# A retention layer and a bilinear feed-forward on one core: seven products for the first tile's last outputs, and an order changed around it

## The chip, the cores and the metric

The kernel runs on one core of a Trainium2 chip. A time is the device time of one execution in microseconds (us); the median of three executions is given. Beside it stands one execution that the hardware profiler recorded, with the start and length of every instruction. Engines are named as the profile names them: PE is TensorE's matmul, PEld its weight load, DVE is VectorE, ACT is ScalarE, POOL is GpSimd, and SP issues the DMAs. All times in the text are counted from the first instruction of the profiled execution, its span.

## The reference

For each of 4 x 8 heads a state of 64 x 64 decays by the head's factor gamma and takes in the outer product of k and v, and q reads it. The result, 3072 tokens of 512 features, goes through two weights whose outputs are multiplied, and through a third weight.

```
state = gamma * state + outer(k[t], v[t]);  y[t] = (q[t] @ state) / 8
x = y as [3072, 512]
out = ((x @ w_a) * (x @ w_b)) @ w_out        # 512 -> 1536 -> 512, float32 in and out
```

## The kernel before

The 768 steps of a sequence are cut into 6 chunks of 128, so there are 24 slots of 128 tokens. The recurrence becomes matmuls: q and k are scaled by a table of powers of gamma, `scores` makes their products within a chunk, a mask cuts them, `intra` applies them to v, `update` adds a chunk to the state, `inter` lets q read it. The first six slots go as three pairs (`casts2`, `flip2`, `scores2`, `update2`, `intra2`, `inter2`, `leave2`): their q and k are transposed on TensorE. From slot 6 on, `casts(t)` scales k and q on GpSimd (`scaled`, L239), casts v (L206), issues a transposing DMA on SP's queue (L254) and then the loads of slot t + 2 (L94, L99). `turn(new, old)` puts scores and state of the slots new, new + 1 and the reads of old, old + 1 on TensorE.

The outputs of the slots are the input of the feed-forward, in tiles of 4, 2, 2, 2, 2, 4 and 8 slots (J = 0 to 6). A tile's 12 blocks of 128 hidden features are each an `a` (L462, w_a, evicted to bf16 by ScalarE, L465) and a `g` (L472, w_b), four matmuls each; VectorE multiplies the two into `ht` (L474). PSUM has three banks under the name `ff` for them. The weights come in six slices that GpSimd casts to bf16 (`cast_w`).

The outputs of a tile come in one of two ways. `ffn_out` (L493) makes one row block of 128 tokens by 12 matmuls of 512 columns. `Group` and `single` make two row blocks together by 7 products of half blocks in place of 8, each of six matmuls of 256 columns (L561), and need sums and differences of the hidden features (`hsum`: `hs` 1 to 4, L503) and of the third weight (`weight_sums`: T1 to T4, L503). TensorE's snapshots of partial sums go out by ScalarE (L568), and VectorE adds them. Before, tile 0 uses the plain way for its four blocks, the later tiles the other. The last tile uses the same seven products for its first two weights too (`Unit`, L698), from sums of the weights that GpSimd makes piece by piece (`weight_pieces`).

Every instruction is chained to the one before on its engine by `seq`, so that the order of the text is the order of each engine's and each DMA queue's work; what is written for different engines runs beside each other, held by semaphores alone. Buffers come from pools with a fixed count (three raw buffers each for k, q and v, three for `kqT`, six `w`), and a load into one waits until its last reader is done. `warm` (L448) multiplies zeros, with no reader, to fill time early on.

Around the change the text before reads (L828 to L836, and L889 to L905):

```
    cast_w(0); W2 = 2 * P
    warm(psff, "ff", 256)
    intra2(1, 0, True); inter2(1)
    ffn_a(0, 0, 0, W2)
    intra2(1, 1, False); leave2(1, (A_, D_))
    ffn_a(0, 1, 0, W2)
    ...
    casts(6); blocks(1, 0, 3); casts(7); blocks(1, 3, NFT)
    outs(0, 0); weight_sums(0, 3); weight_sums(3, 6); outs(0, 1)
    casts(8); outs(0, 2); turn(6, None, V_)
    hsum(1, 3, 0, 6); hsums(1, 0, 6, V_)
    outs(0, 3); casts(9); turn(None, 6); single(1, AT0, AT1, FF)
```

Of the kernel before, what the change touches and what calls it, by code (L numbers as in the profile page):

```python
# [16 lines left out]
PAIRS = 3  # L17


LOADS = "p0 p1 w0 w1 w2 w3 w4 k2 q2 a5 v2 b5 o0 o1 o2 o3 o4 o5 s6 s7".split()  # L20


@with_exitstack
def kernel(
# [10 lines left out]
    nc = tc.nc  # L35
# [44 lines left out]

    raws, wst, whole = {}, {}, {}

    def load_slot(t):
        b, ci = divmod(t, NCH)
        for nm, src in (("k", k), ("q", q), ("v", v)):
# [38 lines left out]
    def issue_loads(n):  # L124
        for _ in range(min(n, len(pending))):
            what = pending.pop(0)
            n = int(what[1:])
            if what[0] in "ab":
                load_w(n, what[0])
            elif what[0] in "kqv":  # L130
                load_two(what[0], {"k": k, "q": q, "v": v}[what[0]], 0, n, 2 * n)
            else:
                {"p": load_pair, "s": load_slot, "w": load_w, "o": load_o}[what[0]](n)


    kqb = {}
# [65 lines left out]
    def cast(engine, dst, src):  # L202
        if engine is nc.scalar:
            seq(nc.scalar.copy(dst, src))
        else:
            seq(engine.tensor_copy(dst, src))  # L206
# [238 lines left out]
    def warm(pool, tag, *cols):  # L445
        idle = pool.tile([P, HP * P], F32, tag=tag, name="idle")
        for n in cols:
            seq(nc.tensor.matmul(idle[:, :n], zero[:, :P], zero[:, :n], start=True, stop=True,  # L448
                                 skip_group_check=True))
# [17 lines left out]
    def ffn_g(J, ft, c0=0, c1=None):  # L467
        c1 = TILES[J] * P if c1 is None else c1
        fs = slice(ft * P, (ft + 1) * P)
        g = psff.tile([P, 4 * P], F32, tag="ff", name="g")[:, : c1 - c0]  # L470
        for kt in range(KT):
            seq(nc.tensor.matmul(g, wb_bf[:, kt, fs], xcols(J, kt, c0, c1),  # L472
                                 start=(kt == 0), stop=(kt == KT - 1)))
        seq(nc.vector.tensor_tensor(ht[J][:, ft, c0:c1], g, asbs.pop((J, ft, c0)), op=ALU.mult))  # L474
# [13 lines left out]
    def ffn_out(J, i):  # L488
        store()
        osb = osbp.tile([P, DM], F32, tag="osb", name="osb")  # L490
        o = psff.tile([P, DM], F32, tag="ff", name="o")
        for ft in range(NFT):
            seq(nc.tensor.matmul(o, ht[J][:, ft, i * P : (i + 1) * P], wo_bf[:, ft],  # L493
                                 start=(ft == 0), stop=(ft == NFT - 1)))
        cast(nc.scalar, osb, o)
        held.append((rows(J, i // 2, i % 2), osb))

    def rows(J, u, r):
        n0 = (sum(TILES[:J]) + 2 * u) * P
        return out[n0 : n0 + 2 * P, :].rearrange("(n r) d -> r n d", r=2)[r]  # L500

    def tt(dst, x, y, op, eng=nc.vector):
        seq(eng.tensor_tensor(dst, x, y, op=op))  # L503

    T1 = []

    def weight_sums(a, b):
        if not T1:
            T1.append(wstage.tile([P, NP, DH], BF16, tag="w", name="wsum1"))
        j = slice(a, b)  # L510
        tt(T3[:, j], B22[:, j], B12[:, j], ALU.subtract)
        tt(T2[:, j], T3[:, j], B11[:, j], ALU.add)
        tt(T4[:, j], B21[:, j], T2[:, j], ALU.subtract)
        tt(T1[0][:, j], B12[:, j], B11[:, j], ALU.subtract)

    hs = {}

    def hsum(J, s, a, b, eng=nc.vector):
        U = 2 if isinstance(J, tuple) else TILES[J] // 2
        if (J, s) not in hs:  # L520
            pool, tag = (raw, ("kf", "qf", "vf", "kf")[s - 1]) if J == (BIG, 1) else (wstage, "w")
            hs[J, s] = pool.tile([P, NP, 2, P], BF16, tag=tag, name=f"hs{s}")
        v = ht[J].rearrange("p (k j) (u r n) -> p r k j u n", k=2, r=2, n=P)
        A11, A12, A21, A22 = (v[:, r, k2, a:b, :U] for r in range(2) for k2 in range(2))
        S = {x: hs[J, x][:, a:b, :U] for x in (1, 2, 3, 4) if (J, x) in hs}
# [335 lines left out]
    scores2(2, 0, "y")  # L861
    scores2(2, 1)
    ffn_a(0, 10)
    update2(2, 0)
    ffn_a(0, 11)
    intra2(2, 0, True)
    inter2(2)
    intra2(2, 1, False)
    leave2(2, (A_, D_))
    ffn_g(0, 10)  # L870
    ffn_g(0, 11)
    for j in range(NO):
        cast_o(j)
# [65 lines left out]
    v_cast(14)  # L939
# [67 lines left out]
```

## Time and profile before

| what | us |
|---|---|
| median of 3 executions (222.5 to 222.67) | 222.5 |
| the profiled execution | 222.53 |
| its span, first to last instruction | 220.8 |
| PE busy in it | 214.2 |
| POOL busy | 140.6 |
| DVE busy | 135.8 |
| ACT busy | 99.2 |

A row of the order of time gives the start in us, the length in us, the engine, the line, the operation, what it writes and reads, the shapes, how many instructions were merged (x4), and in brackets how long the engine stood idle before and what it waited for. Matmuls are pipelined: a row's length holds the drain of its last matmul, and the next row starts before it ends, so the price of a piece is the distance of two starts, or its length in the chain of waits, where overlaps are cut off. A row of the waits gives who waited for what: us in total, how often, the longest. A row of DMA issues gives how many, the KB of each and the median us from issue to landing.

### The profile page before, as it was taken

How to read it: one execution, taken by the hardware profiler on the slowest of the kernel's cores; microseconds unless marked ns; L12 is line 12 of the kernel's file. 1: busy time of each engine (PE TensorE's matmuls, PEld its weight loads, DVE VectorE, ACT ScalarE, POOL GpSimd, SP SyncE). 2: the span in 40 equal slices, each digit the busy share in tenths (PEclk: the TensorE clock that was granted, in tenths of full speed). 3: DMA queues.
4: the chain of work that ended last, by engine and by line, in shares of the span. 5: the costliest groups of instructions: out<-in, count | busy, mean ns of one | idle time of the engine just before them, and what ended most of it. 6: DMA issues, size and time to landing. Idle time of an engine off the chain costs nothing.

```text
span 220.8 us, 5622 instructions
## 1 busy us (share of the span) xinstructions
PE 214.2 (97%) x2233; PEld 144.6 (66%) x2244; DVE 135.8 (61%) x254; ACT 99.2 (45%) x217; POOL 140.6 (64%) x155
## 2 busy tenths in 40 slices
PE   7999999999999999999999999999999999999994
PEld 3567445587458878878888665456865444448883
DVE  3785347745774473566476345776465777789642
ACT  3364333443224444354576344555536656542331
POOL 5364666777554469659846944599999999820000
PEclk9999999999999999999999999999999999999999
DMA  6999999997999999999998599990022000000055
GB/s 170 290 324 348 350 309 342 385 262 164 217 186 286 214 239 240 237 180 274 188 224 219 118 245 194 225 174 3 3 85 105 0 1 3 0 1 4 24 190 166
DMA packets 87194, 39.68 MB, mean 180 GB/s; under 512 B 57472, under 2 KB 82944, under 8 KB 87168
## 3 DMA queue, kind: packets, MB, share of 16 engines
q1 hardware_dynamic: 87024, 39.26, 76.9%
q8 instruction: 17, 0.28, 0.5%
q14 instruction: 9, 0.07, 0.1%
q10 hardware_dynamic: 144, 0.07, 0.1%
HBM read 28.31 MB, written 6.29 MB: 157 GB/s over the span
## 4 chain that ended last, share of the span: by engine, by line
PE 93%; DMA 2%; DVE 2%; issue 1%; ACT 0%; SPq 0%; DVEq 0%; ACTq 0%
PE a L462 19%; PE g L472 19%; PE mA L561 12%; PE uA L698 8%; PE mB L561 6%; PE o L493 5%; PE uB L698 4%; PE mC L561 3%; DMA qf<-in_q_dram 2%; PE at L273 2%; PE y L320 2%; PE uC L698 2%; PE st L290 2%; PE kb L756 2%; PE ka L756 2%; PE y L427 1%
## 5 line engine op out<-in xcount | busy, mean ns | idle before, releaser
L474 DVE TENSOR_TENSOR ht<-g,asb 128x256 bf16<-128x256 f32 (+1 forms) x74 | 37.1, 503 | 40.4 <-PE g L472 34.0
L472 PE MATMUL g<-xt,wb_bf 128*128 128x256 bf16 (+1 forms) x296 | 53.2, 304 | 0.4 <-DVE ht L474 0.4
L462 PE MATMUL a<-xt,wa_bf 128*128 128x256 bf16 (+1 forms) x292 | 53.4, 304 | 0.2
L465 ACT CAST asb<-a 128x256 bf16<-128x256 f32 (+1 forms) x74 | 32.2, 437 | 44.6 <-PE a L462 42.0
L472 PEld LDWEIGHTS <-wb_bf 128*128 128x128 bf16 x296 | 28.8, 98 | 13.4 <-issue 0.7
L239 POOL TENSOR_TENSOR kqb<-kf,ktab 128x512 bf16<-128x512 f32 x22 | 23.2, 1057 | 20.4 <-DMA kf<-in_k_dram 17.3
L462 PEld LDWEIGHTS <-wa_bf 128*128 128x128 bf16 x296 | 27.9, 98 | 12.2 <-issue 0.8
L561 PEld LDWEIGHTS <-hs 128*128 128x128 bf16 x240 | 23.4, 98 | 3.9
L279 DVE TENSOR_TENSOR aT<-at,mask 128x512 bf16<-128x512 f32 x36 | 22.3, 683 | 0.3
L704 ACT COPY snap<-uA 128x512 f32<-128x512 f32 x30 | 16.7, 588 | 12.6 <-PE uA L698 12.0
L239 POOL TENSOR_TENSOR kqb<-qf,qtab 128x512 bf16<-128x512 f32 x18 | 19.2, 1066 | 4.7 <-DMA qf<-in_q_dram 4.7
L503 POOL TENSOR_TENSOR hs<-ht,hs 128x384 bf16<-128x384 bf16 (+1 forms) x17 | 16.6, 982 | 5.8 <-DVE ht L474 5.8
L568 ACT COPY snaps<-mA 128x256 f32<-128x256 f32 x30 | 11.2, 373 | 19.8 <-PE mA L561 19.7
L561 PEld LDWEIGHTS <-ht 128*128 128x128 bf16 x180 | 17.5, 98 | 2.8
L503 POOL TENSOR_TENSOR hs<-ht 128x384 bf16<-128x384 bf16 (+2 forms) x12 | 13.8, 1152 | 3.7 <-DVE ht L474 3.7
L561 PE MATMUL mA<-wsum,hs 128*128 128x256 bf16 x120 | 15.7, 273 | 0.0
L206 POOL CAST vb<-vf 128x512 bf16<-128x512 f32 x16 | 10.1, 643 | 7.3 <-DMA vf<-in_v_dram 7.1
L503 POOL TENSOR_TENSOR ht<-gsb,asb 128x512 bf16<-128x512 bf16 x12 | 13.9, 1169 | 1.3 <-DVE gsb L503 1.3
L503 DVE TENSOR_TENSOR osb<-mB,snaps 128x256 f32<-128x256 f32 x20 | 8.4, 422 | 9.4 <-PE mB L561 5.1
L493 PE MATMUL o<-wo_bf,ht 128*128 128x512 bf16 x46 | 10.6, 380 | 0.1
L331 ACT CAST xt<-y 128x512 bf16<-128x512 f32 x18 | 9.7, 588 | 1.5 <-PE y L320 1.4
L448 PE MATMUL idle<-zero 128*128 128x256 f32 (+2 forms) x16 | 8.2, 632 | 1.6 <-DVE zero L140 1.5
(104 smaller groups left out, 323.0 us busy)
## 6 DMA issues: line engine op xcount, KB each, us to landing
qf<-in_q_dram SPq DMA_DIRECT2D x12, 512.0 KB, 5.7
out_dram<-osb SPq DMA_DIRECT2D x21, 256.0 KB, 3.9
kf<-in_k_dram SPq DMA_DIRECT2D x18, 256.0 KB, 4.6
vf<-in_v_dram SPq DMA_DIRECT2D x18, 256.0 KB, 5.4
wsta<-in_moe_w_a_dram SPq DMA_DIRECT2D x6, 512.0 KB, 8.4
wstb<-in_moe_w_b_dram SPq DMA_DIRECT2D x6, 512.0 KB, 8.1
wsto<-in_moe_w_out_dram SPq DMA_DIRECT2D x6, 512.0 KB, 7.6
kf<-in_k_dram SPq DMA_DIRECT2D x3, 512.0 KB, 7.1
```

Of the source, the lines that this page charges most:

```text
L239: seq(eng.tensor_tensor(dst, src, tab, op=ALU.mult))
L279: seq(nc.vector.tensor_tensor(aT[t][:, r], at[r], mask.to_broadcast([P, HP, P]), op=ALU.mult))
L462: seq(nc.tensor.matmul(a, wa_bf[:, kt, fs], xcols(J, kt, c0, c1), start=(kt == 0), stop=(kt == KT - 1)))
L465: seq(nc.scalar.copy(asb, a))
L472: seq(nc.tensor.matmul(g, wb_bf[:, kt, fs], xcols(J, kt, c0, c1), start=(kt == 0), stop=(kt == KT - 1)))
L474: seq(nc.vector.tensor_tensor(ht[J][:, ft, c0:c1], g, asbs.pop((J, ft, c0)), op=ALU.mult))
L493: seq(nc.tensor.matmul(o, ht[J][:, ft, i * P : (i + 1) * P], wo_bf[:, ft], start=(ft == 0), stop=(ft == NFT - 1)))
L503: seq(eng.tensor_tensor(dst, x, y, op=op))
L561: seq(nc.tensor.matmul(m, w, right[:, j], start=(first and j == 0), stop=(j == NP - 1), skip_group_check=True))
L568: seq(nc.scalar.copy(self.snaps[:, n], self.bank["A"]))
L698: seq(nc.tensor.matmul(m, w, right[:, k], start=(first and k == 0), stop=(k == 1), skip_group_check=True))
L704: seq(nc.scalar.copy(self.snaps[n], self.bank["A"]))
```

## The change

Tile 0's row blocks 2 and 3 are made by `Group(0, 1)`. `ffn_out` is cut into two halves of six matmuls, `weight_sums` into `weight_sum(n)` with two halves each; `hsum` takes tile 0, second pair of blocks alone, with its `hs` in raw buffers and one `kqT` buffer. The hs3 halves stand behind blocks 5 and 6 of tile 0, the others behind the first six blocks of tile 1. Slots 6 and 7 are scaled together (`casts_two`), loads of both in one go, their value casts last. The zeros ahead of `intra2(1, 0)` go; the first two `a` blocks of tile 0 stand there, slices 0 and 1 of the weights are cast in halves, and the first `g` stands behind `update2(1, 1)`. The third pair's transposes, blocks 9 to 11 and attention change places. GpSimd's scaling of slots 13, 15, 16, 18 and 19 stands ahead of sums of `hs`, two of tile 2's sums go to VectorE, and eight weight pieces come sooner.

```diff
-LOADS = "p0 p1 w0 w1 w2 w3 w4 k2 q2 a5 v2 b5 o0 o1 o2 o3 o4 o5 s6 s7".split()
+LOADS = "p0 p1 w0 w1 w2 w3 w4 k2 q2 a5 v2 b5 o0 o1 o2 o3 o4 o5 s6".split()
...
+    def load_slots(t):
+        for u, names in ((t, "kq"), (t + 1, "k"), (t, "v"), (t + 1, "v")):
+            load_slot(u, names)
...
+    def cast_w(j, names="ab", parts=1):
+        n = WC // parts
         for nm, dst in (("a", wa_bf), ("b", wb_bf)):
-            if nm in names:
-                cast(nc.gpsimd, dst[:, :, sl], wst[nm, j])
+            for i in range(parts if nm in names else 0):
+                c = j * WC + i * n
+                cast(nc.gpsimd, dst[:, :, c : c + n], wst[nm, j][:, :, i * n : (i + 1) * n])
...
+    def casts_two(t):
+        for u in (t, t + 1):
+            new_nat(u)
+            scaled(nc.gpsimd, u, 0)
+            scaled(nc.gpsimd, u, 1)
+            flip(u)
+        for u in (t, t + 1):
+            cast(nc.gpsimd, vb[u], raws["v", u])
+        load_slots(t + 2)
...
+    def ffn_out(J, i, n):
+        if n == 0:
+            store()
+            plain_out[i] = psff.tile([P, DM], F32, tag="ff", name="o")
+        o = plain_out[i]
+        for ft in range(NP * n, NP * n + NP):
             seq(nc.tensor.matmul(o, ht[J][:, ft, i * P : (i + 1) * P], wo_bf[:, ft],
...
+    def weight_sum(n):
...
+        for j in (slice(0, NP // 2), slice(NP // 2, NP)):
+            tt(dst[:, j], x[:, j], y[:, j], op)
...
     def hsum(J, s, a, b, eng=nc.vector):
-        U = 2 if isinstance(J, tuple) else TILES[J] // 2
+        U = slice(int(J == 0), 2 if isinstance(J, tuple) else TILES[J] // 2)
...
-    cast_w(0)
+    cast_w(0, parts=2)
     W2 = 2 * P
-    warm(psff, "ff", 256)
+    ffn_a(0, 0, 0, W2)
+    ffn_a(0, 1, 0, W2)
     intra2(1, 0, True)
     inter2(1)
-    ffn_a(0, 0, 0, W2)
     intra2(1, 1, False)
     leave2(1, (A_, D_))
-    ffn_a(0, 1, 0, W2)
+    update2(1, 1)
+    ffn_g(0, 0, 0, W2)
     issue_loads(100)
-    cast_w(1)
-    update2(1, 1)
+    cast_w(1, parts=2)
     ffn_a(0, 0, W2, 2 * W2)
     ffn_a(0, 1, W2, 2 * W2)
-    ffn_g(0, 0, 0, W2)
     ffn_g(0, 1, 0, W2)
...
-        if ft == 7:
-            scaled(D_, 4, Q)
-            scaled(D_, 5, Q)
+        if ft in (5, 6):
+            hsum(0, 3, 3 * ft - 15, 3 * ft - 12)
+    scaled(D_, 4, Q)
+    scaled(D_, 5, Q)
     flip2(2, K, [((0, 1), A_)])
     ffn_a(0, 9)
+    ffn_g(0, 9)
     flip2(2, Q, [((0, 1), D_)], psat, "y0")
-    ffn_g(0, 9)
+    ffn_a(0, 10)
     scores2(2, 0, "y")
     scores2(2, 1)
-    ffn_a(0, 10)
+    ffn_a(0, 11)
     update2(2, 0)
-    ffn_a(0, 11)
+    ffn_g(0, 10)
     intra2(2, 0, True)
     inter2(2)
     intra2(2, 1, False)
     leave2(2, (A_, D_))
-    ffn_g(0, 10)
     ffn_g(0, 11)
...
-    casts(6)
-    blocks(1, 0, 3)
-    casts(7)
-    blocks(1, 3, NFT)
-    outs(0, 0)
-    weight_sums(0, 3)
-    weight_sums(3, 6)
-    outs(0, 1)
+    casts_two(6)
+    for ft in range(NFT):
+        ffn_ab(1, ft)
+        if ft < 6:
+            hsum(0, (2, 1, 4)[ft // 2], ft % 2 * 3, ft % 2 * 3 + 3)
+    g = Group(0, 1, FF, FF, FF)
+    weight_sum(3)
+    weight_sum(2)
+    ffn_out(0, 0, 0)
+    ffn_out(0, 0, 1)
+    weight_sum(1)
     casts(8)
-    outs(0, 2)
-    turn(6, None, V_)
+    g.p1()
+    g.p2()
+    ffn_out(0, 1, 0)
+    turn(6, None)
+    weight_sum(4)
+    g.p7()
     hsum(1, 3, 0, 6)
-    hsums(1, 0, 6, V_)
-    outs(0, 3)
+    g.p6()
+    ffn_out(0, 1, 1)
+    g.p5()
     casts(9)
     turn(None, 6)
+    g.p3()
+    g.p4()
+    hsums(1, 0, 6, V_)
     single(1, AT0, AT1, FF)
...
-    hsums(2, 3, 6, G_)
+    hsum(2, 2, 3, 6, G_)
+    hsum(2, 1, 3, 6)
+    hsum(2, 4, 3, 6)
     casts(13)
...
     blocks(3, 8, 9)
+    casts(15)
     hsums(3, 0, 3, G_)
-    casts(15)
     blocks(3, 9, 10)
     turn(12, 10)
     blocks(3, 10, NFT)
+    casts(16)
     hsums(3, 3, 6, G_)
-    casts(16)
...
     hsum(4, 3, 0, 6, G_)
+    casts(18)
     blocks(4, 6, 8)
     v_cast(16)
     blocks(4, 8, 9)
     hsums(4, 0, 3, G_)
-    casts(18)
...
     blocks(4, 11, NFT)
+    casts(19)
     hsums(4, 3, 6, G_)
-    casts(19)
     single(4, Y0, AT0, FF)
+    v_cast(18)
     casts(20)
-    v_cast(18)
...
     blocks(5, 5, 6)
+    weight_pieces(6)
     turn(18, 16)
...
-    weight_pieces(1)
+    weight_pieces(2)
     turn(20, 18)
```

More of the change, by code (lines that the diff above doesn't have):

```diff
@@ L81, with load_slot @@
     raws, wst, whole = {}, {}, {}
-    def load_slot(t):
+    def load_slot(t, names="kqv"):
         b, ci = divmod(t, NCH)
-        for nm, src in (("k", k), ("q", q), ("v", v)):
+        for nm in names:
+            src = {"k": k, "q": q, "v": v}[nm]
             if nm == "q":
@@ L132, in issue_loads @@
             else:
-                {"p": load_pair, "s": load_slot, "w": load_w, "o": load_o}[what[0]](n)
+                {"p": load_pair, "s": load_slots, "w": load_w, "o": load_o}[what[0]](n)
     kqb = {}
@@ L206, in cast @@
             seq(engine.tensor_copy(dst, src))
-    def cast_w(j, names="ab"):
-        sl = slice(j * WC, (j + 1) * WC)
+    def cast_w(j, names="ab", parts=1):
+        n = WC // parts
         for nm, dst in (("a", wa_bf), ("b", wb_bf)):
-            if nm in names:
-                cast(nc.gpsimd, dst[:, :, sl], wst[nm, j])
+            for i in range(parts if nm in names else 0):
+                c = j * WC + i * n
+                cast(nc.gpsimd, dst[:, :, c : c + n], wst[nm, j][:, :, i * n : (i + 1) * n])
     def cast_o(j):
@@ L251, in casts, with flip @@
             cast(nc.gpsimd, vb[t], raws["v", t])
+        flip(t)
+        if t + 2 < NSLOT:
+            load_slot(t + 2)
+    def flip(t):
         if t % 2 == 0:
@@ L486, in store @@
         held.clear()
[L488 to L492, printed above, removed]
-            seq(nc.tensor.matmul(o, ht[J][:, ft, i * P : (i + 1) * P], wo_bf[:, ft],
-                                 start=(ft == 0), stop=(ft == NFT - 1)))
-        cast(nc.scalar, osb, o)
-        held.append((rows(J, i // 2, i % 2), osb))
+    plain_out = {}
+    def ffn_out(J, i, n):
[4 more added lines that the diff above has]
+        for ft in range(NP * n, NP * n + NP):
+            seq(nc.tensor.matmul(o, ht[J][:, ft, i * P : (i + 1) * P], wo_bf[:, ft],
+                                 start=(ft == 0), stop=(ft == NFT - 1), skip_group_check=True))
+        if n:
+            osb = osbp.tile([P, DM], F32, tag="osb", name="osb")
+            cast(nc.scalar, osb, o)
+            held.append((rows(J, i // 2, i % 2), osb))
     def rows(J, u, r):
@@ L505 @@
     T1 = []
-    def weight_sums(a, b):
-        if not T1:
+    def weight_sum(n):
+        if n == 1:
             T1.append(wstage.tile([P, NP, DH], BF16, tag="w", name="wsum1"))
[L510 to L514, printed above, removed]
+        x, y, op = {3: (B22, B12, ALU.subtract), 2: (T3, B11, ALU.add), 4: (B21, T2, ALU.subtract),
+                    1: (B12, B11, ALU.subtract)}[n]
+        dst = T1[0] if n == 1 else {2: T2, 3: T3, 4: T4}[n]
+        for j in (slice(0, NP // 2), slice(NP // 2, NP)):
+            tt(dst[:, j], x[:, j], y[:, j], op)
     hs = {}
     def hsum(J, s, a, b, eng=nc.vector):
-        U = 2 if isinstance(J, tuple) else TILES[J] // 2
+        U = slice(int(J == 0), 2 if isinstance(J, tuple) else TILES[J] // 2)
         if (J, s) not in hs:
-            pool, tag = (raw, ("kf", "qf", "vf", "kf")[s - 1]) if J == (BIG, 1) else (wstage, "w")
-            hs[J, s] = pool.tile([P, NP, 2, P], BF16, tag=tag, name=f"hs{s}")
+            pool, tag = (raw, ("kf", "qf", "vf", "kf")[s - 1]) if J in (0, (BIG, 1)) else (wstage, "w")
+            bufs = {}
+            if (J, s) == (0, 4):
+                pool, tag, bufs = tra, "kqT", {"bufs": 3}
+            hs[J, s] = pool.tile([P, NP, 2, P], BF16, tag=tag, name=f"hs{s}", **bufs)
         v = ht[J].rearrange("p (k j) (u r n) -> p r k j u n", k=2, r=2, n=P)
-        A11, A12, A21, A22 = (v[:, r, k2, a:b, :U] for r in range(2) for k2 in range(2))
-        S = {x: hs[J, x][:, a:b, :U] for x in (1, 2, 3, 4) if (J, x) in hs}
+        A11, A12, A21, A22 = (v[:, r, k2, a:b, U] for r in range(2) for k2 in range(2))
+        S = {x: hs[J, x][:, a:b, U] for x in (1, 2, 3, 4) if (J, x) in hs}
         x, y, op = {3: (A11, A21, ALU.subtract), 2: (A22, S[3], ALU.subtract), 1: (A21, A22, ALU.add),
```

5 lines of the change are left out of this document (removed).

## The prediction

> **What bounds the kernel now.** I read the page first, for the engine that is never idle, then what that engine waits for, then the chain for the price of its pieces, and at last the order of time around every edit.
>
> ```profile
> span 220.8 us, 5622 instructions
> PE 214.2 (97%) x2233; PEld 144.6 (66%) x2244; DVE 135.8 (61%) x254; ACT 99.2 (45%) x217; POOL 140.6 (64%) x155
> PEclk9999999999999999999999999999999999999999
> PE 93%; DMA 2%; DVE 2%; issue 1%; ACT 0%; SPq 0%; DVEq 0%; ACTq 0%
> ```
>
> TensorE is busy for 97% of the span, at the full granted clock in every slice, and makes 93% of the chain. No other engine passes 64%. Its waits, all of them:
>
> ```profile
> PE idle L448 <- DVE zero L140: 1.5, 1, 1.5
> PE tp L375 <- DVE kqb L239: 0.5, 2, 0.3
> PE g L472 <- DVE ht L474: 0.4, 1, 0.4
> ```
>
> After the first 1.5 us it waits 0.9 us in all. So time can go in two ways only: fewer matmuls, or matmuls that start earlier at the front and are not caught up by a fixed arrival later. And it can come back in one: a stall where there is none now.
>
> **Part 1: seven products for eight.** The price of a matmul is read from the chain, as start-to-start time.
>
> ```profile
> 25.70 0.86 PE a L462 x4
> 199.22 2.62 PE mA L561 x24
> ```
>
> 512 columns cost 0.86/4 = 0.215 us, 256 columns 2.62/24 = 0.109. Two plain blocks are 2 x 12 matmuls of 512 columns: 5.16 us. By products they are 7 x 6 of 256: 4.59. So 0.57 us less, on the path, since TensorE has no idle time there. The two blocks that stay plain are cut in halves around the turn of slots 6 and 7 and keep their count.
>
> What it adds lies on VectorE: eight half sums of `hs` (128 x 384), two in tile 0 and six behind the first six blocks of tile 1; the eight `weight_sum` halves were there already. The transposes of slots 6 and 7 are wanted earlier, because the turn now stands behind one and a half plain blocks and two products, 2.58 + 1.31 + 1.29 = 5.2 us from the start of the outputs, where three blocks (7.7) stood; this is what the joint scaling of 6 and 7 pays for, and SP's queue issues slot 7's transposes straight behind slot 6's instead of behind three loads.
>
> ```profile
> 53.05 1.04 POOL L239 TENSOR_TENSOR kqb<-qf,qtab 128x512 bf16<-128x512 f32 x1
> kqT<-kqb SPq DMA_TRANSPOSE x18, 4.9
> 61.84 0.64 PE L273 MATMUL at<-kqT 64*64 64x128 bf16 x32
> ```
>
> Slot 7's scaling ends one value cast (0.6) and one load's order sooner, at about 53.1; plus 4.9 is 58.0, against scores at 61.84 - 2.6 = 59.2. It is covered by 1.2 us; late by more than that, it would stall every matmul behind it.
>
> The half sums are hidden only if VectorE keeps the pace of a block, 8 matmuls of 256 = 0.87 us.
>
> ```profile
> 46.14 0.42 DVE L474 TENSOR_TENSOR ht<-g,asb 128x256 bf16<-128x256 f32 x1 [0.45 <-PE g L472]
> 65.46 0.85 DVE L503 TENSOR_TENSOR hs<-ht,hs 128x768 bf16<-128x768 bf16 x1
> 66.23 0.55 DVE L503 TENSOR_TENSOR hs<-ht 128x768 bf16<-128x768 bf16 x1
> 64.95 0.94 POOL L206 CAST vb<-vf 128x512 bf16<-128x512 f32 x1
> 43.00 1.04 POOL L206 CAST wo_bf<-wsto 128x1024 bf16<-128x1024 f32 x1 [0.32 <-DMA wsto<-in_moe_w_out_dram]
> ```
>
> No row has 384 elements. 768 take 0.55 with GpSimd idle and 0.85 with GpSimd busy (65.46 stands beside the vb cast of 64.95); half of that is 0.28 to 0.43. I take 0.4, as GpSimd is casting `wo_bf` then; 0.42 + 0.4 = 0.82 is under 0.87, so 0. Were the whole 0.30 of contention added to the half (0.28 + 0.30 = 0.58), a block would take 1.00, and six lose 0.8. [...]
>
> **Part 2: `a` blocks for the zeros, half casts.**
>
> ```profile
> 14.04 1.17 POOL L206 CAST vb<-vf 128x512 bf16<-128x512 f32 x2 [1.46 <-DMA vf<-in_v_dram]
> 15.54 1.04 POOL L206 CAST wa_bf<-wsta 128x1024 bf16<-128x1024 f32 x1 [0.34 <-DMA wsta<-in_moe_w_a_dram]
> 18.49 1.04 POOL L206 CAST wb_bf<-wstb 128x1024 bf16<-128x1024 f32 x1 [1.91 <-DMA wstb<-in_moe_w_b_dram]
> 15.70 0.70 PE L448 MATMUL idle<-zero 128*128 128x256 f32 x2
> 16.33 0.77 PE L427 MATMUL y<-aT,vb 64*64 64x128 bf16 x16
> 17.48 0.60 PE L462 MATMUL a<-xt,wa_bf 128*128 128x256 bf16 x4
> 19.04 0.44 PE L404 MATMUL st<-vb,kqb 64*64 64x64 bf16 x16
> 20.29 1.96 PE L472 MATMUL g<-xt,wb_bf 128*128 128x256 bf16 x16
> 22.08 1.03 PE L462 MATMUL a<-xt,wa_bf 128*128 128x512 bf16 x4
> ```
>
> A half cast is one of the two in 1.17: 0.58, two of them 0.13 longer than the whole. Both weights start when their loads land (15.54, 18.49), which the change does not touch. So the first `a` starts at 15.54 + 0.58 + some 0.06 = 16.18, after 0.48 idle; the second at 16.76, to 17.2; `y` of slots 2 and 3 (0.40 + 0.45 + 0.48) to 18.5; `st` (0.37) to 18.9; the first `g` waits for 18.49 + 0.64 = 19.13. Six groups of 0.447 (1.79/4, from 20.29 to 22.08) end at 21.8: 0.28 ahead of 22.08. Then the third pair:
>
> ```profile
> 32.45 2.04 POOL L239 TENSOR_TENSOR kqb<-kf,ktab 128x512 bf16<-128x512 f32 x2 [0.76 <-DMA kf<-in_k_dram]
> 34.17 0.77 PE L375 MATMUL tp<-ident,kqb 128*128 128x128 bf16 x8
> 38.96 1.04 POOL L206 CAST wb_bf<-wstb 128x1024 bf16<-128x1024 f32 x1 [0.26 <-DMA wstb<-in_moe_w_b_dram]
> 41.37 1.90 PE L472 MATMUL g<-xt,wb_bf 128*128 128x512 bf16 x8
> 43.11 0.60 PE L462 MATMUL a<-xt,wa_bf 128*128 128x256 bf16 x4
> ```
>
> GpSimd starts the k scaling when k lands (32.45) and ends slot 5's at 34.49. The transposes then end at 34.8 whether TensorE comes at 34.17 or at 33.89: the 0.28 is gone there. Behind it stand the same pieces in another order. `g` of block 10 now comes ahead of the second half of the attention, at about 40.1, and its weights are cast at 40.0: a cover of 0.1 where 1.37 was. VectorE takes the q scaling behind block 8's product, and the q copy behind block 9's, so the scores can wait some 0.15, which stays inside that cover's size. I take 0 for the start of tile 1 at 43.11, with both ends kept: 0.28 sooner (nothing catches it) to 0.3 later.
>
> **Part 3: scalings sooner.** GpSimd's order changes, and TensorE feels it only where sums of `hs` come late. In tile 2, two half sums go to VectorE; the one that must wait for GpSimd's sum delays a product of `ht` by some 0.4, and a free bank covers that: 0. In tile 4, slot 18's scaling drops into a hole of GpSimd that is there anyhow, and the queue behind it stands as before: 0. Slots 19 to 23 and eight weight pieces come sooner than their readers need. The narrow place is tile 3:
>
> ```profile
> 96.16 1.64 POOL L503 TENSOR_TENSOR hs<-ht 128x768 bf16<-128x768 bf16 x1 [1.66 <-DVE ht L474]
> 98.82 0.91 POOL L503 TENSOR_TENSOR hs<-ht,hs 128x384 bf16<-128x384 bf16 x1 [1.02 <-DVE ht L474]
> 101.43 1.04 POOL L239 TENSOR_TENSOR kqb<-kf,ktab 128x512 bf16<-128x512 f32 x1
> 103.43 0.91 POOL L503 TENSOR_TENSOR hs<-ht,hs 128x384 bf16<-128x384 bf16 x1
> 105.36 0.82 PE L561 MATMUL mA<-wsum,hs 128*128 128x256 bf16 x6
> 98.14 0.58 SPq L99 DMA_DIRECT2D qf<-in_q_dram  x1
> qf<-in_q_dram SPq DMA_DIRECT2D x12, 512.0 KB, 5.7
> ```
>
> Now the second half of hs2 ends at 104.3 and is read at 105.36. After the change GpSimd does, from 96.16: 1.6 (hs3), 2.0 (slot 15), 2.6 (three half sums), 2.0 (slot 16), 0.9 (hs2): 105.3. All cover is used up. That holds if slot 16's q is in by 103.4; it was issued at 98.14, and 5.7 later is 103.8. The transposes of slot 13 leave one us sooner now and shorten the queue ahead of it, so I take 0; with the old landing it costs 0.4.
>
> **The sum.** 0.57 gained, 0 for the front, 0 for VectorE, 0 for tile 3. The profiled execution took 222.53 us, 1.7 of it around the span, and stands 0.03 over the median 222.5: 222.53 - 0.57 = 221.96, I say 221.95.
>
> **The rivals.**
> - The front's 0.28 also lands: 221.65. For it: TensorE reaches 34.17 early. Against: k, q and the last weights land one behind the other, and their times are not the matmuls' to move.
> - Sums of tile 3 come late by 0.4, since slot 16 now stands ahead of them: 222.4, no change. For it: q's median landing.
> - The other side: VectorE becomes the bound in tile 1's first six blocks. A half sum over 0.45 paces the matmuls; at 0.55 the gain is gone (6 x 0.10), and from 0.62 on (6 x 0.17 = 1.0) the kernel is slower than before by 0.45. At 0.7 it loses 1.5: 223.5. For it: 0.85 beside GpSimd. Against: the 0.55 without it, and casts that leave holes.
> - The clock falls, since real idle time stands where zeros kept TensorE busy.
>
> ```profile
> 1.52 4.63 PE L448 MATMUL idle<-zero 128*128 128x512 f32 x6 [1.52 <-DVE zero L140]
> 10.26 1.12 PE L448 MATMUL idle<-zero 128*128 128x512 f32 x2
> ```
>
>  At the start, 1280 columns of zeros take 4.63 us (3.6 ns each), later 512 take 1.12 (2.2). The same 4.63 us at 2.2/3.6 of the pace lose 1.8: less the 0.57, 223.8. Against: the idle pieces are 0.48 and 0.23. [...]
>
> **How the numbers follow.** What a measurement of this kernel can tell from no change is about 0.2%, 0.45 us: faster is under 222.05, slower over 222.95. Forecast 0.50 (221.75 to 222.3, of which a tenth lies inside "same"); front lands too 0.12; tile 3 late 0.18; VectorE bound 0.11 (two thirds of it slower); clock 0.05; other small stalls 0.04, half of them slower. Faster: 0.45 + 0.12 = 0.57. Slower: 0.07 + 0.05 + 0.02 and some doubt, 0.16. Same: 0.27. The range reaches from the front's gain in full to a lost gain with a 0.4 stall, 221.5 to 222.9; left out are the clock and VectorE at its worst.
>
> **What would show it.** Outputs: plain blocks of tile 0 as 24 matmuls and 42 of 256 columns, and the step from the start of the outputs to the first product of tile 1 shorter by 0.6. Front: an idle TensorE of about 0.5 near 15.7 and 0.2 near 18.9, transposes of k ending at 34.8 again, tile 1 at 43.1. VectorE: half sums at 0.3 to 0.45, and blocks of tile 1 still 0.87 apart. Tile 3: no stall ahead of p6. The prediction is wrong if blocks of tile 1 spread, if `g` of block 10 waits for its weights by more than 0.3, if p6 of tile 3 stalls, or if the granted clock is under 1 before 22 us.

## The result, and the profile after

The changed kernel takes 234.0 us (median; 233.46 to 235.22), the kernel before, beside it on the same chip, 222.51. The ratio is 1.052, with a 95% interval from 1.049 to 1.054: 11.5 us slower, where 0.55 us faster was forecast and 222.9 was the upper end of the range. A ratio in this text is that of the means, and an execution over 1.5% above the fastest of its kernel, as one of the twelve of `e9_sums_behind` was, is left out of it.

The page of the changed kernel, its profiled execution of 234.04:

```profile
span 232.3 us, 5669 instructions
PE 215.5 (93%) x2249; PEld 147.0 (63%) x2260; DVE 145.5 (63%) x266; ACT 100.0 (43%) x220; POOL 140.9 (61%) x157
PEclk9999999995999999999999999999999999999999
PE 82%; DMA 6%; DVE 5%; issue 3%; POOL 1%; ACT 1%; SPq 0%; DVEq 0%; ACTq 0%
```

TensorE's share of the span has gone from 97% to 93% and its share of the chain from 93% to 82%: it waits now. And one slice of the 40, the tenth, has half the clock. TensorE's waits, the longest of them:

```profile
PE a L481 <- DVE ht L493: 7.4, 1, 7.4
...
PE tp L394 <- DVE kqb L245: 1.2, 3, 0.5
PE a L481 <- DVE osb L527: 0.8, 1, 0.8
PE g L491 <- ACT asb L484: 0.7, 1, 0.7
```

One wait of 7.4 us, once, is two thirds of the loss. Where it stands is read from the order of time around it, all engines together:

```profile
45.19 0.42 DVE L493 TENSOR_TENSOR ht<-g,asb 128x256 bf16<-128x256 f32 x1 [0.21 <-PE g L491]
...
46.34 0.60 PE L491 MATMUL g<-xt,wb_bf 128*128 128x256 bf16 x4
...
52.10 1.04 POOL L245 TENSOR_TENSOR kqb<-qf,qtab 128x512 bf16<-128x512 f32 x1
...
53.18 0.73 DVE L527 TENSOR_TENSOR hs<-ht,hs 128x384 bf16<-128x384 bf16 x1 [7.56 <-POOL kqb L245]
...
54.30 1.01 PE L481 MATMUL a<-xt,wa_bf 128*128 128x256 bf16 x4 [7.36 <-DVE ht L493]
...
55.10 1.06 PE L491 MATMUL g<-xt,wb_bf 128*128 128x256 bf16 x4
```

Read it from the bottom: the `a` of tile 1's block 3 waits for a product of `ht`, to give a PSUM bank free. That product stands in VectorE's queue behind the first half sum of tile 0's `hs` 2, and that sum stood idle for 7.56 us until GpSimd had scaled slot 7's q (the row of 52.10). Its inputs, the hidden features, were there; what was not is its output buffer. The pool gave `hs` 2 the raw buffer in which the q of slots 6 and 7 lay, which GpSimd still had to read. With no product made the three banks filled, and TensorE stood: from the start of the `g` at 46.34 to that of the `a` at 54.30 are 7.96 us where two such starts lie 0.44 apart, so 7.5 are lost.

The pool did not hand out the buffer that had been idle longest. In the program as built, `hs` 2 lies at the address of slots 6 and 7's q, while the buffer of slots 4 and 5's q, last read by the scaling that ends at 37.8 (shown below), goes to slot 10's q, whose load is issued later.

The second loss follows from the first. Stretches of 2 us of the changed kernel (busy us of each engine, then the granted clock, the share of the DMA engines and GB/s):

```profile
50.00:52.00 2.00, 0.00 (x0) 0.00 (x0) 0.00 (x0) 0.00 (x0) 1.90 (x2) 1.00 0.82 175
52.00:54.00 2.00, 0.00 (x0) 0.00 (x0) 0.82 (x2) 0.00 (x0) 2.00 (x4) 0.50 0.74 140
56.00:58.00 2.00, 2.00 (x11) 1.40 (x10) 0.71 (x3) 0.37 (x1) 0.00 (x0) 0.50 0.95 233
```

After some 5 us without a matmul the granted clock is 0.50, at 52.0, and it is full again only at 58.8. The half blocks from 54.30 to 58.7 start some 0.85 apart and not 0.44, as the `g` of 55.10 and the next `a` show:

```profile
55.96 1.06 PE L481 MATMUL a<-xt,wa_bf 128*128 128x256 bf16 x4
```

That is some 2.2 us over five half blocks and a part of the sixth. That the clock is the reason is put to the test below (`e5_zeros8`).

The rest is smaller. Tile 1 starts at 44.04 where it started at 43.11, 0.93 late, for two reasons:

```profile
33.90 1.02 PE L491 MATMUL g<-xt,wb_bf 128*128 128x512 bf16 x4 [0.67 <-ACT asb L484]
...
35.64 2.12 DVE L245 TENSOR_TENSOR kqb<-qf,qtab 128x512 bf16<-128x512 f32 x2
35.74 1.48 POOL L211 CAST wa_bf<-wsta 128x1024 bf16<-128x1024 f32 x1 [1.27 <-DMA wsta<-in_moe_w_a_dram]
...
37.82 0.40 PE L394 MATMUL tp<-ident,kqb 128*128 128x128 bf16 x4 [0.50 <-DVE kqb L245]
...
44.04 0.61 PE L481 MATMUL a<-xt,wa_bf 128*128 128x256 bf16 x4
```

`g` of block 8 waits for ScalarE's eviction of block 8's own `a`: as built, it has got the same PSUM bank. And VectorE's scaling of slots 4 and 5's q, which now stands behind block 8's product, meets a cast; the two take 2.12 and 1.48, where they take 1.46 and 1.04 in the kernel before, and the transposes of q wait. In tile 2 a stall of 0.97 is new (the `a` of 98.68 would have started at 97.71, 0.65 behind the six matmuls of 97.06):

```profile
96.17 0.91 POOL L527 TENSOR_TENSOR hs<-ht,hs 128x384 bf16<-128x384 bf16 x1
...
97.11 1.18 DVE L527 TENSOR_TENSOR hs<-ht,hs 128x384 bf16<-128x384 bf16 x1 [1.80 <-POOL hs L527]
...
98.22 0.41 DVE L527 TENSOR_TENSOR osb<-mC,snaps 128x256 f32<-128x256 f32 x1
```

The half sum that was moved to VectorE waits for GpSimd's `hs` 2, then takes 1.18 beside a scaling, and the addition that empties the bank of mC comes behind it. Against all that, the outputs of tile 0 got shorter by 0.3 only (12.23 from their start at 64.35 to 76.58, against 12.54). In sum 7.5 + 2.2 + 0.9 + 1.0 - 0.3 is 11.3; the 0.2 that is left to the 11.5 stays unexplained.

### The profile page after: what moved, and what is told of

It reads as the page before. It is cut to its first block, busy times and chain, and to the rows that moved or that the text cites. A ratio compares the mean times of both kernels' runs of the same rounds, so it can differ in the third digit from the quotient of the medians.

```text
span 232.3 us, 5669 instructions
## 1 busy us (share of the span) xinstructions
PE 215.5 (93%) x2249; PEld 147.0 (63%) x2260; DVE 145.5 (63%) x266; ACT 100.0 (43%) x220; POOL 140.9 (61%) x157
## 4 chain that ended last, share of the span: by engine, by line
PE 82%; DMA 6%; DVE 5%; issue 3%; POOL 1%; ACT 1%; SPq 0%; DVEq 0%; ACTq 0%
PE a L481 18%; PE g L491 17%; PE mA L588 12%; PE uA L725 7%; PE mB L588 6%; DMA qf<-in_q_dram 6%; PE uB L725 4%; PE mC L588 3%; PE at L292 2%; PE y L339 2%; PE uC L725 2%; PE kb L783 1%; PE ka L783 1%; DVE kqb L245 1%; PE st L309 1%
## 5 line engine op out<-in xcount | busy, mean ns | idle before, releaser
L481 PE MATMUL a<-xt,wa_bf 128*128 128x256 bf16 (+1 forms) x292 | 54.6, 309 | 8.9 <-DVE ht L493 7.4
L491 PE MATMUL g<-xt,wb_bf 128*128 128x256 bf16 (+1 forms) x296 | 54.5, 309 | 1.1 <-ACT asb L484 0.7
L481 PEld LDWEIGHTS <-wa_bf 128*128 128x128 bf16 x296 | 28.3, 99 | 22.3 <-issue 9.2
L588 PEld LDWEIGHTS <-hs 128*128 128x128 bf16 x264 | 25.7, 98 | 4.7 <-issue 0.3
L595 ACT COPY snaps<-mA 128x256 f32<-128x256 f32 x33 | 12.3, 373 | 22.3 <-PE mA L588 22.1
L588 PEld LDWEIGHTS <-ht 128*128 128x128 bf16 x198 | 19.4, 98 | 3.2
L527 POOL TENSOR_TENSOR hs<-ht,hs 128x384 bf16<-128x384 bf16 (+1 forms) x16 | 15.8, 990 | 5.3 <-DVE ht L493 5.3
L588 PE MATMUL mA<-wsum,hs 128*128 128x256 bf16 x132 | 17.4, 273 | 0.0
L527 DVE TENSOR_TENSOR osb<-mB,snaps 128x256 f32<-128x256 f32 x22 | 9.2, 422 | 11.0 <-PE mB L588 6.5
L527 DVE TENSOR_TENSOR hs<-ht,hs 128x384 bf16<-128x384 bf16 (+3 forms) x12 | 9.3, 771 | 9.4 <-POOL kqb L245 7.6
L527 DVE TENSOR_TENSOR gsb<-uB,snap 128x512 bf16<-128x512 f32 x10 | 6.9, 686 | 4.2 <-ACT snap L731 3.5
```

Source lines behind the costliest of these rows:

```text
L481: seq(nc.tensor.matmul(a, wa_bf[:, kt, fs], xcols(J, kt, c0, c1), start=(kt == 0), stop=(kt == KT - 1)))
L588: seq(nc.tensor.matmul(m, w, right[:, j], start=(first and j == 0), stop=(j == NP - 1), skip_group_check=True))
L595: seq(nc.scalar.copy(self.snaps[:, n], self.bank["A"]))
```

## The experiments

An edit is to the changed kernel, with those earlier edits that the expectation names (from `e3_pool_sums` on, `e5_zeros8` aside, the new buffer of `e1_buffer` is always among them); each run stands beside the kernel before on the same chip (222.44 to 222.51).

**The buffer.** The first sum gets a buffer that nobody needs any more.

```diff
             if (J, s) == (0, 4):
                 pool, tag, bufs = tra, "kqT", {"bufs": 3}
+            if (J, s) == (0, 2):
+                pool, tag, bufs = tra, "kqT2", {"bufs": 2}
```

> The changed kernel with one edit: the first sum of tile 0 (hs2) takes the buffer in which the second pair's transposed slots stood (last read before 22 us) in place of the buffer of slots 6 and 7's raw q. Theory (buffer): VectorE's wait of 7.56 us at 45.6 is for that buffer alone; TensorE's stall of 7.52 goes, and with it the half clock behind it (2.2): 234.0 - 7.5 - 2.2 = 224.3. Rival (pace): VectorE cannot make a half sum and a product of ht within a block of 0.87 us, the stall only turns into six slow blocks: with half sums of 0.7 beside GpSimd's scalings 225.8, more if they take longer. Rival (port): VectorE is kept out by GpSimd, whatever buffer it writes: about 234.

Measured: 225.6 (225.51 to 225.76), 8.4 less, and the clock is full in every slice. So the stall and the clock behind it hung on this one buffer, and the rival of the port falls. But 1.3 of the expected 9.7 did not come. The rows of `e1_buffer` around tile 1's first blocks say why:

```profile
45.53 0.35 DVE L527 TENSOR_TENSOR hs<-ht,hs 128x384 bf16<-128x384 bf16 x1
...
47.11 1.04 POOL L211 CAST wo_bf<-wsto 128x1024 bf16<-128x1024 f32 x1 [0.34 <-DMA wsto<-in_moe_w_out_dram]
...
47.38 0.98 DVE L527 TENSOR_TENSOR hs<-ht 128x384 bf16<-128x384 bf16 x1
...
48.37 1.04 POOL L245 TENSOR_TENSOR kqb<-kf,ktab 128x512 bf16<-128x512 f32 x1 [0.21 <-PE a L481]
...
48.62 1.00 DVE L527 TENSOR_TENSOR hs<-ht 128x384 bf16<-128x384 bf16 x1
```

A half sum takes 0.35 in a hole of GpSimd's and about 1.0 where it starts behind an instruction of GpSimd's: it ends 0.2 after that one does (48.36 behind 48.15, 49.62 behind 49.41). With the product of 0.42 this is over the 0.87 of a block, and tile 1's twelve blocks take 11.2 (44.03 to 55.25) where they took 10.62. The rival of the pace is thus true as well, at 0.6 here. Another 0.7 is in tile 0's last product, whose bank VectorE frees 1.0 late and not 0.3: ahead of that its weight sum T4 meets two scalings, and tile 1's hs3 a cast.

**The clock.** Zeros keep TensorE busy while it waits; the wait itself stays.

```diff
     for ft in range(NFT):
+        if ft == 3:
+            warm(psat, "at0", *[512] * 33)      # e5_zeros8: 8
         ffn_ab(1, ft)
```

> The changed kernel with 33 matmuls of zeros on a bank that nobody uses then, ahead of the a that stalls in tile 1 (block 3). 33 x 0.215 = 7.1 us, so they fit into the stall of 7.52. Theory (clock): the blocks from 54.3 to 58.7 are slow because TensorE stood still; with zeros they take 0.44 a half block again and the kernel takes 234.0 - 2.2 = 231.8, the stall itself unchanged. Rival (backlog): they are slow because VectorE and ScalarE catch up after the stall: 234.0, and the granted clock stays where it was.

Measured: 252.25. The zeros were mis-sized: a matmul of float32 zeros with 512 columns took 0.858 us (28.3 for 33), four times the 0.215 of bf16, so TensorE came back 20.8 us late with VectorE's queue long empty, and the run does not tell the two apart. Eight zeros fit the stall.

> As e2_zeros, with 8 zeros in place of 33: in e2_zeros one of 512 columns took 0.858 us and not 0.215 (28.3 us for 33), so 8 are 6.9 and fit into the stall of 7.52. Theory (clock): with TensorE busy through the stall the blocks behind it take 0.44 a half block and not 0.85, the kernel 234.0 - 2.2 = 231.8. Rival (backlog of VectorE and ScalarE behind the stall): 234.0.

Measured: 233.42 (232.93 to 233.77). The order of time and one stretch of `e5_zeros8`:

```profile
46.74 7.03 PE L467 MATMUL idle<-zero 128*128 128x512 f32 x16
54.18 0.60 PE L481 MATMUL a<-xt,wa_bf 128*128 128x256 bf16 x4 [0.41 <-DVE ht L493]
54.61 0.60 PE L491 MATMUL g<-xt,wb_bf 128*128 128x256 bf16 x4
```

```profile
56.00:58.00 2.00, 2.00 (x21) 1.78 (x19) 1.45 (x6) 0.81 (x3) 0.00 (x0) 1.00 0.97 238
```

The stall stays (the `a` comes at 54.18), the clock is 1.00, and the half blocks stand 0.43 apart. Tile 1 ends at 62.04 where it ended at 64.35: 2.3 earlier, as the theory of the clock had it, and no backlog. The kernel as a whole gains 0.6 only: 0.5 of the 2.3 goes in the outputs (a wait of 0.8 for VectorE's `osb`), the last matmuls start 1.8 earlier, and in this profiled execution the stores behind them end only 1.1 earlier. So the 2.2 is shown by the blocks and not by the time of the kernel, where 231.8 was expected.

**Tile 2's sums.** The two half sums go back to GpSimd.

```diff
-    hsum(2, 2, 3, 6, G_); hsum(2, 1, 3, 6); hsum(2, 4, 3, 6)
+    hsums(2, 3, 6, G_)
```

> e1_buffer, and tile 2's two half sums of hs1 and hs4 are made on GpSimd again. Theory: the stall of 0.97 at 97 us in tile 2 comes from VectorE's half sum of hs4, which waits for GpSimd's hs2 and is slowed by a scaling; it goes: 0.9 less than e1_buffer, 223.4. Rival: GpSimd is then later with its own sums, and p6 or p3 of tile 2 or slot 13's scaling stalls by as much: same as e1_buffer, 224.3.

Measured: 224.89 (223.88 to 225.16), 0.7 less than `e1_buffer`, and the wait for `osb` of 0.8 is gone from the list. So 0.7 of the stall of 0.97 comes back as time, and the rival of a late GpSimd falls.

**The front.** First the place of tile 0's two half sums of hs3, and with it the bank.

```diff
-        if ft in (5, 6):
+        if ft in (7, 8):        # first half behind block 7, second behind 8
```

> e3_pool_sums, and the two half sums of hs3 of tile 0 stand behind blocks 7 and 8 in place of 5 and 6; with this order g of block 8 gets another PSUM bank than its own a. Theory (bank): the stall of 0.84 ahead of that g goes; the transposes of k still wait for GpSimd until 34.8, so 0.4 of it lands: 223.0 if e3 is 223.4. Rival (order): what makes tile 1 start 0.93 later is VectorE's q scaling behind block 8's product beside a cast (2.12 for 1.46), now another half sum later: no gain or 0.3 more than e3.

Measured: 224.40 (224.31 to 225.15). The wait of `g` for `asb` is gone, and tile 1 starts at 43.55, 0.4 earlier than in `e3_pool_sums` (43.97): the theory of the bank. In the program as built `g` of block 8 now has another bank than its `a`. The other half of the 0.93 is still there. Then the third pair's old order:

```diff
-    scaled(D_, 4, Q); scaled(D_, 5, Q)      # behind block 8
+        if ft == 7: scaled(D_, 4, Q); scaled(D_, 5, Q)
     (and: g 9 behind the transposes of q, a 10 and a 11 one place later, g 10 behind leave2)
```

> e4_bank with the third pair in the order of the kernel before (q scaling behind block 7, g of block 10 behind the attention). Theory (order): in e4 the a blocks of 9 and 10 stand 0.4 and 0.3 at the third pair's transposes, since VectorE's q scaling is late and meets a cast; the old order takes these away, and tile 1 starts at 43.1 where it started at 43.54: 224.4 - 0.4 = 224.0. Rival (start): the a blocks in place of zeros and the half casts make tile 1 late: 224.4.

Measured: 224.52 (224.44 to 224.91): nothing gained, where 0.4 was expected, and tile 1 starts at 43.52. The rival named the right time for a wrong reason: the `a` blocks do not make tile 1 late (see `e8_all` below). The order of time of VectorE in `e6_third_order` shows what took the place of the removed wait:

```profile
35.55 0.35 DVE L527 TENSOR_TENSOR hs<-ht 128x384 bf16<-128x384 bf16 x1
35.82 0.68 DVE L493 TENSOR_TENSOR ht<-g,asb 128x512 bf16<-128x512 f32 x1
36.42 0.59 DVE L527 TENSOR_TENSOR hs<-ht 128x384 bf16<-128x384 bf16 x1
36.93 0.68 DVE L211 COPY kqT<-tp 128x1024 bf16<-128x1024 bf16 x1
```

The half sums now stand ahead of the copy of q's transposes, and the scores wait 0.6 for that. In none of the three orders tried (the change's, `e4_bank`'s and this one) do the two half sums fit in beside the third pair without a delay.

**The sums on GpSimd.** On top of the last one, tile 0's hs2, hs1 and hs4 move to GpSimd's idle time.

```diff
     casts_two(6)
+    for s in (2, 1, 4):
+        hsum(0, s, 0, 6, G_)
     for ft in range(NFT):
         ffn_ab(1, ft)
-        if ft < 6:
-            hsum(0, (2, 1, 4)[ft // 2], ft % 2 * 3, ft % 2 * 3 + 3)
```

> e6_third_order, and tile 0's hs2, hs1 and hs4 are made on GpSimd, in its idle time of 5 us behind the casts of slots 6 and 7, in place of VectorE's half sums behind tile 1's first six blocks. Theory (pace): these six half sums, 0.34 alone and 0.9 to 1.2 beside an instruction of GpSimd, spread tile 1's blocks from 10.62 to 11.7; without them the blocks take 10.62 again: 1.1 less than e6, 222.9. Rival: GpSimd's sums (about 5.2) meet VectorE's weight sums, the first product waits, and the gain is given back: same as e6, 224.0.

Measured: 227.11 (226.7 to 228.19). Tile 1's twelve blocks take 10.62 (43.41 to 54.03) where they took 11.73 in `e6_third_order`, 1.1 less, which settles the pace. But the rival came, larger than it was priced. Rows and one wait of `e7_sums_on_pool`:

```profile
54.15 1.64 POOL L527 TENSOR_TENSOR hs<-ht,hs 128x768 bf16<-128x768 bf16 x1
54.65 3.47 DVE L527 TENSOR_TENSOR wsum<-wo_bf 128x768 bf16<-128x768 bf16 x2
55.74 1.95 POOL L527 TENSOR_TENSOR hs<-ht 128x768 bf16<-128x768 bf16 x1
```

```profile
PE mB L590 <- DVE osb L527: 3.1, 1, 3.1
```

```profile
64.00:66.00 2.00, 2.00 (x11) 1.41 (x10) 2.00 (x5) 0.00 (x0) 2.00 (x3) 0.50 0.86 174
```

Two weight sums that take 1.02 alone take 3.47 beside GpSimd's sums; each ends 0.4 after one of these does. TensorE stood 3.1 us, and after that the granted clock was 0.50 too, from 63.5 to 66.9 by the pace of the matmuls. The same once more, with all four sums on GpSimd:

```diff
+    for s in (3, 2, 1, 4):
+        hsum(0, s, 0, 6, G_)        # and none of hs3 in tile 0
...
+    hsum(1, 3, 0, 6)
     weight_sum(3)
...
-    hsum(1, 3, 0, 6)                # was behind p7
```

> e7_sums_on_pool, with hs3 of tile 0 on GpSimd too (ahead of the other three), and tile 1's hs3 ahead of the weight sums in place of behind the second product. Theory: the stall of 1.0 ahead of the last product of tile 0 (mB waits for VectorE's osb, which stands behind a weight sum and hs3 that both meet scalings) goes, and what is left of the change is its 0.57: 222.9 - 1.0 = 221.9, under the kernel before. Rival: GpSimd is 6.8 us behind with slots 8 and 9, and VectorE's sums are late for the first product: 222.9 or more.

Measured: 229.59 (229.03 to 229.72); the rival again, TensorE waits 5.7 us there. One thing of use: without sums in tile 0, with the old order and with the `a` blocks in place of the zeros, tile 1 starts at 43.10, where the kernel before starts it at 43.11.

**The sums in a quiet place.** GpSimd waits for its next slot's k from 54.4 on, for about 4 us. All of VectorE's sums go there.

```diff
+    for n in (3, 2, 1):
+        hsum(0, n, 0, 6)
+        weight_sum(n)
     ffn_out(0, 0, 0); ffn_out(0, 0, 1); casts(8); g.p1(); g.p2()
+    hsum(0, 4, 0, 6)
...
     g.p5()
+    hsum(1, 3, 0, 6)
```

> Tile 0's seven products kept, but its half sums stand neither in tile 0, nor behind tile 1's first blocks, nor on GpSimd: VectorE makes hs3, T3, hs2, T2, hs1, T1 behind tile 1's last block, where GpSimd waits for its next slot (54.4 to 59.5), then hs4 ahead of the masks and tile 1's hs3 behind p5. Third pair in the old order, tile 2's sums on GpSimd. Theory (turns): two-input sums of VectorE are slow only because they take turns with GpSimd's instructions; without these they are 4.8 us in all and end before 59.5, no product waits, tile 1 starts at 43.1 and its blocks take 10.6: what is left is 7 products for 8, 222.5 - 0.57 = 221.95, under the kernel before. Rival (VectorE full): this place has no 5 us of VectorE to give, the first products wait for hs3 or hs2, or the masks come late: 222.5 or more.

Measured: 222.34 (221.91 to 225.78), ratio 1.0008 (0.9986 to 1.0029); the profiled execution 222.05. VectorE in `e9_sums_behind`:

```profile
54.23 0.55 DVE L527 TENSOR_TENSOR hs<-ht 128x768 bf16<-128x768 bf16 x1
54.69 1.02 DVE L527 TENSOR_TENSOR wsum<-wo_bf 128x768 bf16<-128x768 bf16 x2
55.63 0.55 DVE L527 TENSOR_TENSOR hs<-ht,hs 128x768 bf16<-128x768 bf16 x1
56.10 1.02 DVE L527 TENSOR_TENSOR wsum<-wsum,wo_bf 128x768 bf16<-128x768 bf16 x2
57.03 0.55 DVE L527 TENSOR_TENSOR hs<-ht 128x768 bf16<-128x768 bf16 x1
...
58.16 1.26 POOL L245 TENSOR_TENSOR kqb<-kf,ktab 128x512 bf16<-128x512 f32 x1 [3.82 <-DMA kf<-in_k_dram]
```

The same sums, each at its price alone while GpSimd stands idle (the 3.82 in its row), and no product of tile 0 waits, as the theory of turns forecast, and the rival of a full VectorE falls. `hs` 4, which comes at 58.77 beside GpSimd's next scaling, takes 1.06 again. The median is 0.4 over the expected 221.95. The third pair's new order, alone on top of this:

```diff
-        if ft == 7: scaled(D_, 4, Q); scaled(D_, 5, Q)
+    scaled(D_, 4, Q); scaled(D_, 5, Q)      # behind block 8, and the rest of the order as in the change
```

> e9_sums_behind with the third pair in the order of the change (q scaling behind block 8's product, g of block 10 ahead of the second half of the attention), and no sum near it. Theory (order costs): VectorE's q scaling starts behind block 8's product at 34.9 and meets the cast of the last wa piece at 35.7, the transposes of q wait, tile 1 starts 0.3 to 0.4 later than in e9: 222.3. Rival (the prediction's 0): the pieces are the same and a wait of 0.15 stays in the cover: as e9.

Measured: 222.29 (222.02 to 224.33), as `e9_sums_behind`. In the profiles tile 1 starts at 43.38 and not at 43.00, 0.4 later, as the theory of the order had it, but only 0.16 of it is left at the last products, because in `e9_sums_behind` tile 3's p6 waits 0.18 for GpSimd in return. The executions scatter by more than that, so the time alone cannot tell the two readings apart.

**Which part carries the gain.** The scalings go back to their old places, and then the front too, so that only the seven products, the order of tile 0's outputs and the joint scaling of slots 6 and 7 are left of the change.

```diff
-    casts(15); hsums(3, 0, 3, G_)
+    hsums(3, 0, 3, G_); casts(15)
     (slots 16, 18, 19, 20 and the weight pieces likewise; e12 also: cast_w(0), the zeros and the first a and g blocks as before)
```

> e9_sums_behind with the scalings of slots 13 to 21 and the weight pieces where the kernel before has them. The profiled execution of e9 took 222.05, a third of its others 223 to 226. Theory (cover): the earlier scaling of slot 16 leaves no cover ahead of tile 3's p6 (0.2 us of stall in e9's profile); with the old places that stall goes and the executions lie together: 221.9, none over 222.6. Rival (other): the scatter comes from the outputs of tile 0 or from the front: still above 223 in some, median 222.3. Rival (no effect of the scalings either way): 222.05.

Measured: 221.96 (221.7 to 223.36), ratio 0.999 (0.9969 to 1.001). The median is the expected one, and the stall ahead of tile 3's p6 is gone from the profile, but "none over 222.6" failed: two of seven executions took 222.93 and 223.36. More is told by the span of each execution, from its first instruction to its last. These two have spans of 220.1 and 220.3, the other five 220.0 to 220.2: they lost their time outside. In `e9_sums_behind` four of twelve spans are 221.3 to 224.1, in `e10_new_third` two of twelve are 221.7 and 222.6, and of the sixteen of `e11_old_scalings` and `e12_seven_alone` none is over 220.5. So the scatter inside the span comes and goes with the sooner scalings; by which wait is open, since no scattered execution was profiled.

> The kernel before with only seven products for eight in tile 0, its sums placed as in e9, and slots 6 and 7 scaled together: neither the a blocks in place of zeros nor the third pair's order nor the sooner scalings. Theory (the prediction's sum): Part 1 alone carries the gain, 0.57, and the start of the front gives nothing because the transposes of k wait for GpSimd until 34.8: 221.9, as e11. Rival: the 0.28 of the front lands in e11 after all: e12 is 222.15 where e11 is 221.9. Rival: Part 1 costs elsewhere: 222.5.

Measured: 221.84 (221.73 to 222.24), ratio 0.9974 (0.9964 to 0.9984): 0.6 us faster than the kernel before, the only version here that beats it beyond the interval. The outputs of tile 0, before and in `e12_seven_alone`, from the order of time:

```profile
53.73 7.93 PE L493 MATMUL o<-wo_bf,ht 128*128 128x512 bf16 x35
...
66.27 0.83 PE L561 MATMUL mA<-wo_bf,ht 128*128 128x256 bf16 x6
```

```profile
53.68 2.75 PE L515 MATMUL o<-wo_bf,ht 128*128 128x512 bf16 x11
...
65.52 0.82 PE L590 MATMUL mA<-wo_bf,ht 128*128 128x256 bf16 x6
```

12.54 has become 11.84. Its list of TensorE's waits is short again:

```profile
PE idle L467 <- DVE zero L145: 1.5, 1, 1.5
PE tp L394 <- DVE kqb L245: 0.6, 2, 0.4
PE g L491 <- DVE ht L493: 0.3, 1, 0.3
```

`e11_old_scalings`, which differs from it by the front alone, is not told apart from it (221.96 against 221.84); tile 1 starts at 43.06 here. So the `a` blocks in place of the zeros and the half casts give nothing that shows, as the prediction had it. No run has the joint scaling of slots 6 and 7 alone; that the gain is that of the products is read from the place where it arises, the outputs of tile 0.

## Why the prediction was wrong

- **7 products for 8, 0.57: right.** In `e12_seven_alone`, where nothing that was added waits, the gain is 0.61, and 0.70 in the outputs themselves; the 0.13 over the sum stays unexplained. The count of matmuls by their start-to-start time was a sound term.
- **The step that failed: "What it adds lies on VectorE", costed at 0.** It asked how long the half sums take and not when each may start. A sum must wait for its inputs and for its output buffer; the prediction looked at the first alone, though the change puts `hs` into raw buffers. The last reader of that buffer, slot 7's q scaling, ends at 53.1 in the prediction's own working, and the first sum comes behind the first block of a tile that starts at 43.1 there: a wait of some 8 us could have been bounded from these two, as the case in which the pool gives out the buffer of slots 6 and 7. With the half clock behind it, it is 9.7 of the 11.5; another buffer for this one sum gave back 8.4 of them (`e1_buffer`).
- **"Half of that is 0.28 to 0.43, I take 0.4": too small.** The size beside GpSimd is not the half of 0.85. In `e1_buffer` and `e4_bank` a half sum that starts while GpSimd is at work lasts until 0.2 after the end of GpSimd's instruction: 0.50 to 1.19 for 384 elements in `e4_bank`, against 0.34 in a hole. So the six half sums lose 0.6 (`e1_buffer`) to 1.1 (`e4_bank`), near the price of the rival "VectorE becomes the bound" (1.0), which was right in mechanism and had a chance of 0.11. The prediction worked out such a price from its rows, the whole 0.30 added to the half of 0.55 and 0.8 lost by all six, and yet took the half for its sum.
- **The front, 0: right in what was reasoned, wrong in what was left out.** The first `a` started at 16.41 (16.18 forecast), the first `g` at 19.11 (19.13), block 2 at 21.84 (21.8). The gain was gone at the transposes of k, which end at 34.78 in `e4_bank`; `e8_all` starts tile 1 at 43.10. What was left out are the two half sums of hs3 on VectorE in that stretch, and that they change which bank a block gets: 0.4 of the 0.93 by the bank (`e4_bank`). And the third pair's order was put too low: "some 0.15" for the scores is 0.4 in `e10_new_third`, which has the order and no sum near it.
- **"A free bank covers that: 0" for tile 2: wrong, 0.7 to 1.0.** It was priced as a wait of 0.4; the sum also met a scaling, and behind it stood the addition that gives the bank free.
- **Tile 3, 0: right in the changed kernel, in part by luck.** There GpSimd's second half of hs2 ends at 116.55 and p6 starts at 116.86. `e9_sums_behind`, which reaches this place without the lost time, stalls 0.18 there: the cover was as thin as the prediction said, and the time lost ahead of it hid that.
- **The rival of the clock: right mechanism, wrong place and price.** It was set at the start, where TensorE waits 0.46 ahead of the first `a`, and there the blocks keep their full pace (two half blocks from 19.65 to 20.53, at a granted clock of 1.00). The clock fell to 0.50 in the stall of 7.4 that the prediction did not see, and stayed at 1.00 with zeros in it (`e5_zeros8`). Its price, too, came from the row of a single matmul of zeros, 1.12 for 512 columns (2.2 ns each): 33 in a row take 0.858 each (1.7 ns) in `e2_zeros`.

## What to carry to other kernels

For an added instruction, ask for three times and not for one: when its inputs are there, when its output buffer's last reader is done, and who stands behind it in its queue; on an engine that empties PSUM, the last can make any wait TensorE's wait, as VectorE's 7.56 became TensorE's 7.36 here. A sum of two SBUF tensors on VectorE was cheap here only where GpSimd stood idle (0.34 for 384 elements, against 0.50 to 1.19, `e4_bank`), so look for GpSimd's holes; sums on both engines at once cost more than on one (two weight sums 3.47 for 1.02 in `e7_sums_on_pool`), and so did the split of tile 2's sums in the change (0.7 us, `e3_pool_sums`). Where a pool chooses buffers or banks, a small insertion elsewhere can change which one an instruction gets: look it up in the program as built.

## What the runs showed of the hardware

- In three runs the granted clock fell to 0.50 in a long stall of TensorE's. In the changed kernel it fell 5.1 us into the stall of 7.4 (52.0) and was back 6.8 later (58.8); in `e7_sums_on_pool` it fell at 63.5, 3.1 into the stall and at its end, and was back 3.4 later by the pace of the matmuls; in `e8_all` 2.9 into a stall of 5.7 (63.0), back 6.8 later by that pace. Behind a wait of 1.0 (`e1_buffer`) it stayed at 1.00. The granted clock reads 1.00 at the very start as well, though a matmul of 512 float32 zeros takes 1.7 us there (by its weight loads, 3.38 to 5.09 in the kernel before) and 0.86 in `e2_zeros`: the row does not show that slow stretch.
- VectorE's sums of two SBUF tensors took longer beside GpSimd's instructions and ended after them: 3.47 for 1.02 (weight sums beside sums, `e7_sums_on_pool`), each 0.4 after one of GpSimd's, and 0.50 to 1.19 for 0.34 (half sums, `e4_bank`), 0.2 after. The products of 256 columns into `ht`, which read `g` from PSUM, took 0.41 to 0.42 in the same stretch of `e4_bank`, beside GpSimd or not. Once both lost: in the changed kernel VectorE's scaling took 2.12 and the cast beside it 1.48, where they take 1.46 and 1.04 in the kernel before.
- A wait cost more than it lasted: in `e7_sums_on_pool` 3.1 us of waiting cost TensorE another 1.7 at half clock (63.5 to 66.9), where six matmuls of 256 columns took 1.23 from start to start (63.51 to 64.74) and 0.66 ahead of the stall (56.62 to 57.28).
